# Attention, gated convolution layer and mixture of experts on one core: the weighted sums of every pair of heads as uncut float32 products

## The chip, the cores and the metric

The kernel runs on one core of a Trainium2 chip. The metric is the device time of one execution in microseconds; of several runs the median is given.

## What is computed

Three layers follow one another on 4 batches of 448 positions. Cut to what matters:

```python
attn = softmax(causal(q @ k.T / 8))          # 4 batches x 12 heads, 448 x 448, head size 64
x    = (attn @ v) laid out as 448 x 768      # attention
h    = relu(x @ w_in)                        # 768 -> 1024
x    = (h * sigmoid(conv3(h))) @ w_out       # 1024 -> 768
# 4 experts, each one head of size 64; the two best of each position count
q, k, v = x @ wq[e], x @ wk[e], x @ wv[e]
ye   = softmax(causal(q @ k.T / 8)) @ v @ wo[e]
out += gate(x)[e] * ye
```

Two heads (or two experts) are worked on together and are called a pair. There are 24 pairs in the attention (6 for each batch) and 8 among the experts (2 for each batch), 32 in all. Each has 448 x 448 causal weights a head, of which the lower triangle of blocks is computed.

## The kernel before, in words

`w_out` is folded into the experts' weights, so the products on TensorE are: x by `w_in`, the fold, the experts' q, k, v, the scores, the weighted sums and the output. All but a few of them are "cut": an operand is split into a high part in the type float32r and a low part (`high`, L604 to L608, and `low`, L612), and a product is the sum of three single-pass products, high by high, low by high and high by low (`products`, L951).

For a pair the scores go by four groups of queries (64, 128, 128 and 128 of them; `Q0`, `QN`). `scores` (L680) runs the two heads at once, each in one half of the array's rows, into the two PSUM tiles `sx` and `sy`. VectorE takes the maximum and the mask (L656), ScalarE the exponential (L660), and the weights are divided by their sum (`norms`, L702, L705) in the tile `e`.

Then the weights are turned by TensorE (`tr`, L714, 16 turns of 128 x 128 for a pair) and multiplied by v. There are two ways:

* `weigh_both` (L758), for the first 8 pairs of the attention (`WHOLE_AV`). The weights of both heads stand interleaved in blocks of 64 keys, v stands in a block-diagonal tile (64 keys of one head above 64 keys of the other), and seven uncut float32 products of 448, 384, 320, 256, 192, 128 and 64 columns give both heads at once. The turned weights are copied out of PSUM four times, and the sum is taken out of `po` as a high part and a low part (two instructions).
* `transpose`, `weigh` and `gather` (L772, L784), for the other 16 pairs of the attention and the 8 of the experts. The 64 keys that stand first are stacked for high and low (`a0`), the 384 others are blocks of 128 keys (`a1`, 768 columns). For each head the turned weights are cut into high and low, v too, and seven single-pass products follow (448, 256, 384, 128 columns, then 128 and 256 with 64 columns of v, then 384). High by high and low by high stand in two halves of `po`; ScalarE copies one half out, VectorE adds the other (L784), and `gather` cuts the sum of both heads into high and low again.

What sets the order of all work is a planner (`Plan`): every instruction is entered with the engines that may do it and a cost, the planner gives each a rank by its longest way to the end, adds the noise of the table `SHIFTS` to the ranks in stretches of the plan, and writes the instructions out in the order of its simulated run. TensorE works strictly in that order. `QUOTA`, `SIZE` and `Kind` say how many buffers of a kind there are: `work` is one SBUF area of 11 units of 2 KB for each partition, from which loads, copies and results are taken.

Of the kernel before, what the change touches and what calls it, by code (L numbers as in the profile page):

```python
# [43 lines left out]
PLACE = (0, 1, 4, 2, 5, 3, 6)  # L44
# [4 lines left out]
SIZE = {"t1": 2, "raw": 2, "wt": 2, "wxr": 2, "wraw": 3}  # L49
PAIRS, THOUS, UNITS, SLABS = 18, 4, 11, 3  # L50
QUOTA = {"xs": 7, "qks": 4, "y": 4, "vs2": 2, "w1": 3, "wraw": 1}
# [114 lines left out]
class Plan:  # L166
# [135 lines left out]
    def run(self):  # L302
# [29 lines left out]
        for seed, lo, hi, amp in SHIFTS:  # L332
            for o in self.ops:
                if lo <= begin[o.n] < hi:
                    rank[o.n] += amp * noise(seed, o.n)
# [147 lines left out]
def on_vector2(n):  # L483
# [4 lines left out]
ON = {"a0": ("AV", "A", "A"), "a1": ("AV", "A", "A"), "x high": ("AVG", "VG", "V"), "x low": ("VG", "G", "VG"),  # L488
      "qk high": ("AVG", "AVG"), "qk low": "VG", "v high": ("V", "AG"), "gx": "AG", "w high": "AVG", "w low": "VG"}
# [34 lines left out]
def attention_moe_moe(ctx: ExitStack, tc: tile.TileContext, qk, vv, w_in, cw, w_out, wqk, wvg, wo, out):  # L524
# [38 lines left out]
    blocks = tiles("block", 2, [128, 7, 2, 64], F32)  # L563
    for t in blocks:
        for o in range(2):
            nc.gpsimd.memset(t[HALF[1 - o], :, o], 0.0)
# [6 lines left out]
    thou = Kind(tiles("thou", THOUS, [128, 1024], F32R))  # L573
# [9 lines left out]
    for name, kind, quota in (  # L583
            ("xs", pairs, QUOTA["xs"]), ("g", pairs, 8), ("qks", pairs, QUOTA["qks"]), ("wx", pairs, 12),
            ("y", pairs, QUOTA["y"]), ("q2", pairs, 2), ("k2", pairs, 2),
            ("vs", thou, 2), ("gx", thou, 1), ("vs2", thou, QUOTA["vs2"]), ("w1", slabs, QUOTA["w1"]), ("wraw", half, QUOTA["wraw"]), ("wt", half, 2), ("wxr", half, 2), ("raw", half, 1),
            ("xf", half, 3), ("xc", half, 2), ("cv", half, 3), ("o", half, 3), ("gw", half, 1),
            ("hp", Kind(hps), 2), ("st", Kind(stats), 4),
            ("e", Kind(tiles("e", 2, [128, 2048], F32)), 2), ("vb", bk, 2), ("kb", bk, 1), ("ab", half, 4),
            ("a0", Kind(tiles("a0", 2, [128, S], F32R)), 2), ("a1", Kind(tiles("a1", 1, [128, 2, 768], F32R)), 1),  # L590
            ("vraw", half, 1), ("qw", half, 1),
# [28 lines left out]
    def scores(qk, j, e, turns=False):  # L620
# [13 lines left out]
        def blocked(ap):  # L634
            return ap.rearrange("p (j d) -> p j d", d=64) if turns else ap

# [3 lines left out]
        def ec(o, c):  # L640
            n = Q0[c] + QN[c]
            if turns:
                return e[:QN[c], COL2[c]:COL2[c] + 2 * n].rearrange("p (j o d) -> p j o d", o=2, d=64)[:, :, o]
            return e[:QN[c], COL2[c] + o * n:COL2[c] + o * n + n]

        def kc(o, c):
            n = Q0[c] + QN[c]
            return slice(0, n) if o or turns else slice(S - n, S)

        def weight(o, c):  # L650
# [3 lines left out]
            def mx(_):  # L654
                m = mask[rows, 448 - w:448] if c and (o or turns) else mask[rows, 320:320 + w]
                nc.vector.tensor_tensor_reduce(out=ec(o, c), in0=blocked(bank(o, c)), in1=blocked(m), scale=-0.125, scalar=3.0e38,  # L656
                                               op0=OP.add, op1=OP.min, accum_out=st[rows, 0, c:c + 1])
# [8 lines left out]
        if whole:  # L666
            for o, (qs, kh, r) in enumerate(qk):
                for c in ORDER:
                    w = Q0[c] + QN[c]
                    P.op({"T": 4 * w / 2400}, lambda _, o=o, c=c, w=w, qs=qs, kh=kh: nc.tensor.matmul(  # L670
                        bank(o, c), qs()[:, Q0[c]:Q0[c] + QN[c]], kh()[:, :w // 64], start=True, stop=True), r=r, w=[(sbs[o][c], c)])
                    weight(o, c)
        else:
            q, k, r = qk
            for two in (ORDER[:2], ORDER[2:]):
# [6 lines left out]
                P.op({"T": 0.09 + sum(3 * max(product(Q0[c] + QN[c]), QN[c] / 1200) for c in two)}, mm, r=r,  # L682
# [33 lines left out]
    def transpose(e, p):  # L716


        ph, t0 = 2 if p >= B * NP else int(p >= NP), P.buf("t0")
        a0, a1 = [P.buf("a0") for _ in range(2)], []  # L720
        for c in range(4):
            tr(lambda c=c: t0[:, Q0[c]:Q0[c] + 128], lambda n=COL2[c] + Q0[c] + QN[c]: e[:, n - 64:n + 64],
               [(e, (o, c)) for o in range(2)], [(t0, c)], QN[c])
        src = [(t0, c) for c in range(4)]
        for o in range(2):
            a, own, oth = a0[o], HALF[o], HALF[1 - o]
            P.op(psum_cost(S, ON["a0"][ph]), high(lambda a=a, own=own: a[own], lambda own=own: t0[own, :S]), r=src, w=[(a, 0)])
            P.op({"V": on_vector(S)}, low(lambda a=a, oth=oth: a[oth], lambda own=own: t0[own, :S], lambda a=a, own=own: a[own]),
                 r=src + [(a, 0)], w=[(a, 1)])
        for o in range(2):  # L730
            t1, a = P.buf("t1"), P.buf("a1")
            for i, (c, k) in enumerate(((1, 1), (2, 1), (3, 1), (3, 3), (2, 2), (3, 2))):
                m = COL2[c] + (Q0[c] + QN[c] + Q0[k] if o else Q0[c] - Q0[k])
                tr(lambda t1=t1, n=128 * i: t1[:, n:n + 128], lambda m=m: e[:, m:m + 128], [(e, (o, c))], [(t1, i + 1)])
            src = [(t1, i) for i in range(1, 7)]
            P.op(psum_cost(768, ON["a1"][ph]), high(lambda a=a: a[:, 0], lambda t1=t1: t1[:, :768]), r=src, w=[(a, 0)])
            P.op({"V": on_vector(768)}, low(lambda a=a: a[:, 1], lambda t1=t1: t1[:, :768], lambda a=a: a[:, 0]), r=src + [(a, 0)], w=[(a, 1)])
            a1.append(a)
        return list(zip(a0, a1))

    def weigh_both(e, v, v_r, dst):


        ps = P.buf("po")
        for i, use in enumerate(BLOCKS):
            t, a = P.buf("tb" if i in (1, 2) else "ta"), P.buf("ab")
            n = 0
            for j, col, q in use:
                for c in range((j + 1) // 2, 4):
                    m = COL2[c] + j * 128  # L750
                    tr(lambda t=t, x=col + Q0[c] - q: t[:, x:x + 128], lambda m=m: e[:, m:m + 128], [(e, (o, c)) for o in range(2)],
                       [(t, (j, c))], QN[c])
                n = col + S - q
            P.op(psum_cost(n, "AV"), high(lambda a=a, n=n: a[:, :n], lambda t=t, n=n: t[:, :n]),
                 r=[(t, (j, c)) for j, _, _ in use for c in range((j + 1) // 2, 4)], w=[(a, 0)])
            for j, col, q in use:
                P.op({"T": max(4 * (S - 64 * j) / 2400, 0.214)},
                     lambda _, a=a, j=j, x=col + 64 * j - q, y=col + S - q: nc.tensor.matmul(  # L758
                         ps[:, 64 * j:S], v(PLACE[j]), a[:, x:y], start=j == 0, stop=j == 4), r=[(a, 0)] + v_r, w=[(ps, 0)])
# [3 lines left out]
    def weigh(a, v, v_r, o, xf):  # L763

        a0, a1 = a
        ps, xc = P.buf("po"), P.buf("xc")
        every, vh = slice(0, 128), HALF[0]

        def mm(q, k, m, rhs, key, start=False, stop=False):
            n = m.stop - m.start  # L770
            P.op({"T": product(S - q)},
                 lambda _: nc.tensor.matmul(ps[:n, q:S], v(k, m), rhs(), start=start, stop=stop),  # L772
                 r=key + v_r, w=[(ps, 0)], m=n)

        mm(0, 0, every, lambda: a0[:, :], [(a0, 0), (a0, 1)], start=True)
        mm(192, 2, every, lambda: a1[:, 0, 512:768], [(a1, 0)])
# [439 lines left out]
```

## Time and profile before

| | |
|---|---|
| median of 3 runs | 577.5 us (577.44 to 579.41) |
| the profiled execution | 578.15 us, of which the span of the instructions is 576.4 us |
| PE (matmuls) busy | 554.0 us, 96% |
| DVE busy | 474.1 us, 82% |
| ACT busy | 396.9 us, 69% |
| POOL busy | 179.8 us, 31% |
| DMA queue of the loads | 37.5% of the 16 engines |

PE is TensorE's matmuls, PEld its weight loads, DVE VectorE, ACT ScalarE, POOL GpSimd, SP the queue that issues the DMAs. Matmuls are pipelined: a record lasts from its start until its last result is out, so the records of neighbours overlap, and the pace is read from start to start. An uncut float32 product leaves two matmul records of its width, a cut one a record for each of its parts.

### The profile page before, as it was taken

How to read it: one execution, taken by the hardware profiler on the slowest of the kernel's cores; microseconds unless marked ns; L12 is line 12 of the kernel's file. 1: busy time of each engine (PE TensorE's matmuls, PEld its weight loads, DVE VectorE, ACT ScalarE, POOL GpSimd, SP SyncE). 2: the span in 40 equal slices, each digit the busy share in tenths (PEclk: the TensorE clock that was granted, in tenths of full speed). 3: DMA queues.
4: the chain of work that ended last, by engine and by line, in shares of the span. 5: the costliest groups of instructions: out<-in, count | busy, mean ns of one | idle time of the engine just before them, and what ended most of it. 6: DMA issues, size and time to landing. Idle time of an engine off the chain costs nothing. (4 is left out here: it accounts for less than half of the span.)

```text
span 576.4 us, 10560 instructions
## 1 busy us (share of the span) xinstructions
PE 554.0 (96%) x3549; PEld 474.3 (82%) x3552; DVE 474.1 (82%) x1318; ACT 396.9 (69%) x1033; POOL 179.8 (31%) x236
## 2 busy tenths in 40 slices
PE   8899999899999999999998999999999899999896
PEld 4688888788789998899897878899888778999775
DVE  5996796799997499986799998973999999845883
ACT  3794563377996496863699998953877978634663
POOL 3141201021541274500249766402337452000010
PEclk9999999999999999999999999999989999999999
DMA  9653504865475011546023263650022414610042
GB/s 264 215 150 102 181 1 130 277 177 196 155 266 134 0 51 55 172 161 209 2 54 99 70 215 100 221 193 1 1 66 86 141 54 164 219 55 2 17 134 97
DMA packets 44086, 70.45 MB, mean 122 GB/s; under 512 B 12672, under 2 KB 35072, under 8 KB 44032
## 3 DMA queue, kind: packets, MB, share of 16 engines
q1 hardware_dynamic: 44032, 69.78, 37.5%
q8 instruction: 28, 0.46, 0.3%
q14 instruction: 26, 0.21, 0.1%
HBM read 56.40 MB, written 13.37 MB: 121 GB/s over the span
## 5 line engine op out<-in xcount | busy, mean ns | idle before, releaser
L951 PE MATMUL pf<-pair,slab 128*128 128x448 f32 (+2 forms) x984 | 217.3, 367 | 4.6 <-DVE wqks L612 2.1
L951 PEld LDWEIGHTS pf<-pair,slab 128*128 128x128 f32 x984 | 171.8, 188 | 25.0 <-DVE wqks L612 2.8
L660 ACT ACTIVATE e<-e,stat 128x320 f32<-128x320 f32 (+3 forms) x256 | 127.2, 499 | 24.2 <-DVE stat L656 23.4
L714 PE MATMUL t<-ident,e 128*128 128x128 f32 (+1 forms) x512 | 86.1, 279 | 3.5 <-DVE e L705 1.1
L951 PE MATMUL pf<-pair,wqks 128*128 128x448 f32 x384 | 80.5, 368 | 0.0
L612 POOL TENSOR_TENSOR pair<-work,pair 128x448 fp32r<-128x448 f32 (+1 forms) x55 | 66.3, 1214 | 45.4 <-DVE pair L606 29.0
L612 DVE TENSOR_TENSOR a<-t,a 64x448 fp32r<-64x448 f32 (+1 forms) x96 | 75.5, 787 | 4.8 <-ACT a L604 2.7
L951 PEld LDWEIGHTS pf<-pair,wqks 128*128 128x128 f32 x384 | 71.7, 188 | 6.4 <-DVE pair L612 0.2
L714 PEld LDWEIGHTS t<-ident,e 128*128 128x128 f32 (+1 forms) x512 | 60.2, 140 | 19.7 <-issue 4.4
L604 ACT ACTIVATE a<-t 64x448 fp32r<-64x448 f32 (+1 forms) x96 | 64.2, 673 | 17.0 <-PE t L714 11.6
L772 PE MATMUL po<-a,thou 128*128 128x384 f32 (+5 forms) x336 | 62.8, 310 | 2.4 <-DVE work L784 1.4
L656 DVE CUSTOM_DVE_ANT_0 e<-sx,mask 128x448 f32<-128x448 f32 (+3 forms) x128 | 51.7, 413 | 1.8 <-PE sy L680 0.8
L656 DVE CUSTOM_DVE_ANT_0 e<-sy,mask 128x192 f32<-128x192 f32 (+3 forms) x128 | 51.2, 414 | 2.4 <-PE sy L680 1.2
L772 PEld LDWEIGHTS po<-a,thou 128*128 128x128 f32 (+1 forms) x336 | 47.0, 175 | 6.9 <-DVE work L784 2.8
L680 PE MATMUL sx<-pair,pair 64*128 64x448 f32 (+3 forms) x280 | 50.6, 295 | 0.3 <-DVE stat L656 0.2
L680 PE MATMUL sy<-pair,pair 64*128 64x448 f32 (+3 forms) x280 | 50.2, 294 | 0.2 <-DVE stat L656 0.2
L660 ACT ACTIVATION_READ_ACCUMULATOR e<-e,stat 128x1 f32 (+1 forms) x256 | 48.4, 189 | 0.0
L612 DVE TENSOR_TENSOR pair<-pf,pair 128x448 fp32r<-128x448 f32 (+3 forms) x32 | 15.5, 502 | 38.8 <-ACT pair L604 38.6
L980 DVE SCALAR_TENSOR_TENSOR work<-hp,cws,work 128x448 f32<-128x448 f32 x64 | 45.7, 722 | 1.8 <-ACT work L975 1.1
L702 ACT ACTIVATE e<-e,stat 128x448 f32<-128x448 f32 (+3 forms) x94 | 42.2, 503 | 6.9 <-DVE stat L698 4.1
L680 PEld LDWEIGHTS sx<-pair,pair 64*128 64x128 f32 (+1 forms) x280 | 40.2, 172 | 6.2 <-DVE stat L656 1.5
L951 PE MATMUL pf<-wvs,pair 128*128 128x260 f32 x288 | 43.2, 295 | 0.4 <-DVE thou L612 0.4
(118 smaller groups left out, 872.7 us busy)
## 6 DMA issues: line engine op xcount, KB each, us to landing
slab<-w_scratch SPq DMA_DIRECT2D x24, 768.0 KB, 4.5
work<-in_w_out SPq DMA_DIRECT2D x8, 768.0 KB, 4.9
work<-in_w_in SPq DMA_DIRECT2D x8, 768.0 KB, 5.8
w_scratch<-slab SPq DMA_DIRECT2D x8, 768.0 KB, 4.3
out<-work SPq DMA_DIRECT2D x24, 224.0 KB, 2.0
slab<-wo_scratch SPq DMA_DIRECT2D x6, 768.0 KB, 4.5
work<-in_vv SPq DMA_DIRECT2D x16, 256.0 KB, 2.9
work<-in_qk SPq DMA_DIRECT2D x17, 224.0 KB, 4.2
```

The source lines that it names most:

```text
L604: nc.scalar.activation(dst(), src(), AF.Copy)
L612: return lambda e: engine(e).tensor_sub(dst(), src(), f32(h()))
L656: nc.vector.tensor_tensor_reduce(out=ec(o, c), in0=blocked(bank(o, c)), in1=blocked(m), scale=-0.125, scalar=3.0e38, op0=OP.add, op1=OP.mi ...
L660: nc.scalar.activation(ec(o, c), ec(o, c), AF.Exp, bias=st[rows, 0, c:c + 1], scale=-1.0, accum_out=st[rows, 1, c:c + 1])
L680: nc.tensor.matmul(bank(o, c), q(s)[own, Q0[c]:Q0[c] + QN[c]], k(t)[own, kc(o, c)], start=i == 0, stop=i == 2)
L702: nc.scalar.activation(ec(o, c), ec(o, c), AF.Copy, scale=st[:QN[c], 3, c:c + 1])
L714: P.op({"T": TURN}, lambda _: nc.tensor.transpose(dst()[:, :n], src()[:n], ident[:n, :n]), r=r, w=keys)
L772: lambda _: nc.tensor.matmul(ps[:n, q:S], v(k, m), rhs(), start=start, stop=stop),
L951: nc.tensor.matmul(out_ap(), a(), b(), start=first, stop=end), r=r, w=[(ps, 0)])
L980: return lambda _: nc.vector.scalar_tensor_tensor(cv[:, :S], hp[:, i:S + i], cws[:, fc, i:i + 1], cv[:, :S], op0=OP.mult, op1=OP.add)
```

## The change

All 32 pairs take one new way, also called `weigh`. `transpose`, the old `weigh`, `gather` and `weigh_both` go.

* The first 64 keys of both heads stay together, as one uncut product of 448 columns with a block-diagonal v (128 rows: 64 keys of one head, 64 of the other).
* The other 384 keys are three blocks of 128 keys for each head. Each block is one uncut float32 product with 64 columns of v, of 384, 128 and 256 moving columns. The two heads write to partitions 0 to 63 and 64 to 127 of `po`, that is, they stand beside each other in the array's columns. These six products are one entry of the plan, which waits for all copies of the weights.
* The turned weights are copied once (448 columns, and three times 512), v isn't cut but loaded straight into its place (three DMAs, no copies), and the sum is taken out of `po` once, as high and low.
* v of the experts is copied from PSUM uncut.
* q and k of all pairs but the first come by the four loads that the cut pairs had (pairs 1 to 7 had one); the first pair's k comes by three loads instead of two, with two POOL memsets.
* The `work` area grows from 11 to 19 units, `thou` (four tiles of 4 KB) gives way to one `gx` tile and six v tiles of 2 KB, `a0` and `a1` go.
* The plan's price for a scores group rises from 0.09 to 0.27 beside its columns, the new entry has `SWITCH` = 0.2, and `SHIFTS` is another table, which can also raise the ranks of a run of entries by a constant: the order of all instructions is new.

```diff
-WHOLE_AV = range(8)
-BLOCKS = (((0, 0, 0),), ((1, 0, 64), (5, 384, 320)), ((2, 0, 64), (6, 384, 320)), ((3, 0, 192), (4, 256, 192)))
+TILES = (((0, 1, 1), (0, 2, 1), (0, 3, 1), (0, 3, 3)), ((1, 1, 1), (1, 2, 1), (1, 3, 1), (1, 3, 3)), ((0, 2, 2), (0, 3, 2), (1, 2, 2), (1, 3, 2)))
+SWITCH = 0.2
...
-PAIRS, THOUS, UNITS, SLABS = 18, 4, 11, 3
+PAIRS, VALUES, UNITS, SLABS, EN = 18, 6, 19, 3, 2
...
+    def weigh(e, v, v_r, dst):
+        ps, n0 = P.buf("po"), P.buf("ab")
+        t = P.buf("ta")
         for c in range(4):
+            tr(lambda c=c: t[:, Q0[c]:Q0[c] + 128], lambda n=COL2[c] + Q0[c] + QN[c]: e[:, n - 64:n + 64],
+               [(e, (o, c)) for o in range(2)], [(t, c)], QN[c])
+        P.op(psum_cost(S, "AV"), high(lambda: n0[:, :S], lambda: t[:, :S]), r=[(t, c) for c in range(4)], w=[(n0, 0)])
+        ab = []
+        for i, use in enumerate(TILES):
+            t, a = P.buf("ta" if i == 2 else "tb"), P.buf("ab")
+            for j, (o, c, k) in enumerate(use):
                 m = COL2[c] + (Q0[c] + QN[c] + Q0[k] if o else Q0[c] - Q0[k])
+                tr(lambda t=t, n=128 * j: t[:, n:n + 128], lambda m=m: e[:, m:m + 128], [(e, (o, c))], [(t, j)])
+            P.op(psum_cost(512, "AV"), high(lambda a=a: a[:, :], lambda t=t: t[:, :]), r=[(t, j) for j in range(4)], w=[(a, 0)])
+            ab.append(a)
+        P.op({"T": 4 * S / 2400}, lambda _: nc.tensor.matmul(ps[:, :S], v[:, 0].rearrange("p o d -> p (o d)"), n0[:, :S], start=True, stop=False),
+             r=[(n0, 0)] + v_r, w=[(ps, 0)])
+        def rest(_):
+            for k, part in ((1, lambda o: ab[o][:, :384]), (3, lambda o: ab[o][:, 384:]), (2, lambda o: ab[2][:, 256 * o:256 * o + 256])):
+                for o, own in enumerate(HALF):
+                    nc.tensor.matmul(ps[own, Q0[k]:S], v[:, k, o], part(o), start=False, stop=k == 2)
+        P.op({"T": 4 * 768 / 2400 + SWITCH}, rest, r=[(a, 0) for a in ab] + v_r, w=[(ps, 0)])
         P.op(psum_cost(S, "AV"), high(lambda: dst[:, 0], lambda: ps[:, :S]), r=[(ps, 0)], w=[(dst, 0)])
         P.op({"V": on_vector(S)}, low(lambda: dst[:, 1], lambda: ps[:, :S], lambda: dst[:, 0]), r=[(ps, 0), (dst, 0)], w=[(dst, 1)])
...
+    def values(p):
+        vb = P.buf("vs")
+        for o in range(2):
+            P.op(dma_cost(16384, 256), load(lambda o=o: vb[HALF[o], 0, o], vv[p, HALF[o], 0, o]), w=[(vb, o)])
+        P.op(dma_cost(196608, 1536), load(lambda: vb[:, 1:], vv[p, :, 1:]), w=[(vb, 2)])
+        return vb, [(vb, i) for i in range(3)]
```

## Rows read from the trace of the kernel before

**Rows 1.** The page: busy time of the engines; the DMA queue; the loads of v.

```profile
PE 554.0 (96%) x3549; PEld 474.3 (82%) x3552; DVE 474.1 (82%) x1318; ACT 396.9 (69%) x1033; POOL 179.8 (31%) x236
...
q1 hardware_dynamic: 44032, 69.78, 37.5%
...
work<-in_vv SPq DMA_DIRECT2D x16, 256.0 KB, 2.9
```

**Rows 2.** Busy time by window: us, then PE, PEld, DVE, ACT, POOL busy, clock, DMA.

```profile
250.00:300.00 50.00, 50.00 (x327) 45.31 (x325) 39.30 (x104) 32.16 (x78) 10.06 (x17) 1.00 0.29 96
300.00:350.00 50.00, 47.32 (x351) 40.80 (x352) 47.43 (x159) 48.02 (x136) 37.75 (x48) 1.00 0.37 119
...
400.00:450.00 50.00, 47.06 (x359) 41.25 (x357) 44.74 (x134) 38.94 (x111) 21.89 (x30) 0.97 0.14 45
```

**Rows 3.** The chain that ended last: start, us, what; a long run of cut products.

```profile
485.73 37.70 PE pf L951 x186
```

**Rows 4.** Timeline of PE: start, us, line, shape, count; an uncut pair, then turns.

```profile
120.93 3.30 PE L758 MATMUL po<-work,block 128*128 128x448 f32 x14
123.94 3.74 PE L951 MATMUL pf<-pair,slab 128*128 128x448 f32 x17
...
164.21 1.04 PE L714 MATMUL t<-ident,e 128*128 128x128 f32 x8
```

**Rows 5.** Groups of PE by form: count, busy us, mean ns of a record, idle before.

```profile
L951 PE MATMUL pf<-pair,slab 128*128 128x448 f32 x696 | 159.8, 375 | 2.5 <-ACT hp L969 0.7 <-DVE pair L606 0.7 <-ACT work L604 0.7
L951 PE MATMUL pf<-pair,wqks 128*128 128x448 f32 x384 | 80.5, 368 | 0.0
L714 PE MATMUL t<-ident,e 128*128 128x128 f32 x480 | 80.3, 279 | 3.5 <-DVE e L705 1.1 <-DVE a L612 1.1 <-POOL e L705 0.7
...
L951 PE MATMUL pf<-wvs,pair 128*128 128x260 f32 x288 | 43.2, 295 | 0.4 <-DVE thou L612 0.4
...
L951 PE MATMUL pf<-pair,slab 128*128 128x512 f32 x144 | 39.9, 412 | 2.1 <-DVE wqks L612 2.1
```

**Rows 6.** Timeline of PE: one head's cut sum, then a visit of the scores.

```profile
304.19 1.08 PE L772 MATMUL po<-a,thou 128*128 128x448 f32 x7
305.11 1.24 PE L951 MATMUL pf<-wvs,pair 128*128 128x260 f32 x9
306.28 0.41 PE L680 MATMUL sx<-pair 64*128 64x320 f32 x1
306.28 0.41 PE L680 MATMUL sy<-pair 64*128 64x320 f32 x1
306.53 0.30 PE L680 MATMUL sx<-pair,pair 64*128 64x320 f32 x1
...
306.68 0.31 PE L680 MATMUL sx<-pair,pair 64*128 64x320 f32 x1
...
307.02 0.27 PE L680 MATMUL sx<-pair,pair 64*128 64x192 f32 x1
...
307.23 0.33 PE L714 MATMUL t<-ident,e 128*128 128x128 f32 x1
```

**Rows 7.** The page's costliest groups: cutting the turned weights, busy us and mean ns.

```profile
L612 DVE TENSOR_TENSOR a<-t,a 64x448 fp32r<-64x448 f32 (+1 forms) x96 | 75.5, 787 | 4.8 <-ACT a L604 2.7
...
L604 ACT ACTIVATE a<-t 64x448 fp32r<-64x448 f32 (+1 forms) x96 | 64.2, 673 | 17.0 <-PE t L714 11.6
```

**Rows 8.** Groups by form: sums out of `po` (cut, uncut), and an uncut copy.

```profile
L784 DVE TENSOR_TENSOR work<-po,work 64x448 f32<-64x448 f32 x48 | 29.4, 613 | 6.8 <-ACT work L604 6.0
L604 ACT ACTIVATE work<-po 64x448 f32<-64x448 f32 x48 | 25.9, 540 | 13.9 <-PE po L772 11.7 <-issue 1.4
...
L604 ACT ACTIVATE work<-t 128x512 f32<-128x512 f32 x15 | 8.5, 593 | 3.3 <-PE t L714 2.0 <-PE po L758 0.7 <-DVE work L606 0.6
...
L612 DVE TENSOR_TENSOR pair<-po,pair 128x448 fp32r<-128x448 f32 x8 | 4.9, 616 | 0.1
...
L604 ACT ACTIVATE pair<-po 128x448 fp32r<-128x448 f32 x6 | 3.3, 543 | 4.7 <-PE po L758 4.7
```

More of the change, by code (lines that the diff above doesn't have):

```diff
@@ L617, in attention_moe_moe, with scores @@
     NORM = {}
-    def scores(qk, j, e, turns=False):
+    def scores(qk, j, e):
         whole = isinstance(qk, list)
@@ L647, in kc @@
             n = Q0[c] + QN[c]
[L648 removed]
+            return slice(0, n) if o else slice(S - n, S)
         def weight(o, c):
@@ L654, in mx @@
             def mx(_):
-                m = mask[rows, 448 - w:448] if c and (o or turns) else mask[rows, 320:320 + w]
-                nc.vector.tensor_tensor_reduce(out=ec(o, c), in0=blocked(bank(o, c)), in1=blocked(m), scale=-0.125, scalar=3.0e38,
+                m = mask[rows, 448 - w:448] if c and o else mask[rows, 320:320 + w]
+                nc.vector.tensor_tensor_reduce(out=ec(o, c), in0=bank(o, c), in1=m, scale=-0.125, scalar=3.0e38,
                                                op0=OP.add, op1=OP.min, accum_out=st[rows, 0, c:c + 1])
@@ L680, in mm @@
                                 nc.tensor.matmul(bank(o, c), q(s)[own, Q0[c]:Q0[c] + QN[c]], k(t)[own, kc(o, c)], start=i == 0, stop=i == 2)
-                P.op({"T": 0.09 + sum(3 * max(product(Q0[c] + QN[c]), QN[c] / 1200) for c in two)}, mm, r=r,
+                P.op({"T": 0.27 + sum(3 * max(product(Q0[c] + QN[c]), QN[c] / 1200) for c in two)}, mm, r=r,
                      w=[(sbs[o][c], c) for c in two for o in range(2)])
@@ L787, in gather, with prepare @@
-    def gather(xf, dst, ph):
-        both = [(xf, 0), (xf, 1)]
-        P.op(copy_cost(S, ON["x high"][ph]), high(lambda: dst[:, 0], lambda: xf[:, :S]), r=both, w=[(dst, 0)])
-        P.op(two_cost(S, ON["x low"][ph]), low(lambda: dst[:, 1], lambda: xf[:, :S], lambda: dst[:, 0]), r=both + [(dst, 0)], w=[(dst, 1)])
     turned = ((lambda ap: ap[:, :384].rearrange("p (b c) -> p b c", b=3), lambda ap: ap[:, 64:].rearrange("p (b c) -> p b c", b=3)[:, ::-1]),
               (lambda ap: ap[:, 384:], lambda ap: ap[:, :64]))
-    def prepare(p, ph, turn):
+    def prepare(p, ph):
@@ L803, in both @@
             return raw[:, :2 * S].rearrange("p (a s) -> p a s", a=2)
-        if turn:
-            P.op(dma_cost(229376, 1792), load(lambda: raw[:, :S], qk[p, :, 0]), w=[(raw, 0)], hold=[hi, lo])
-            P.op(dma_cost(114688, 1792), load(lambda: raw[64:, S:2 * S], qk[p, 64:, 1]), w=[(raw, 1)])
-            for i, (d, q) in enumerate(turned):
-                P.op(dma_cost(86016 - 57344 * i, 512 - 256 * i), load(lambda d=d: d(raw[:64, S:2 * S]), q(qk[p, :64, 1])), w=[(raw, 2 + i)])
-        else:
-            P.op(dma_cost(458752), load(both, qk[p]), w=[(raw, i) for i in range(4)], hold=[hi, lo])
+        P.op(dma_cost(229376, 1792), load(lambda: raw[:, :S], qk[p, :, 0]), w=[(raw, 0)], hold=[hi, lo])
+        P.op(dma_cost(114688, 1792), load(lambda: raw[64:, S:2 * S], qk[p, 64:, 1]), w=[(raw, 1)])
+        for i, (d, q) in enumerate(turned):
+            P.op(dma_cost(86016 - 57344 * i, 512 - 256 * i), load(lambda d=d: d(raw[:64, S:2 * S]), q(qk[p, :64, 1])), w=[(raw, 2 + i)])
         src = [(raw, i) for i in range(4)]
@@ L827, in prepare_whole, with side @@
         P.op(dma_cost(229376, 1792), load(lambda: qw[:, :S], qk[p, :, 0]), w=[(qw, 0)])
+        def side(o):
+            return kb[:, o * S:(o + 1) * S]
         for o in range(2):
-            P.op(dma_cost(114688, 256), load(lambda o=o: kb[HALF[o], :, o], qk[p, HALF[o], 1].rearrange("p (j d) -> p j d", d=64)), w=[(kb, o)])
-        return [(lambda: qw[:, :S], lambda o=o: kb[:, :, o], [(qw, 0), (kb, o)]) for o in range(2)]
-    def values(p, ph):
-        raw, vs = P.buf("vraw"), P.buf("vs")
-        def whole():
-            return raw[:, :].rearrange("p (c o d) -> p c o d", c=4, o=2)
-        P.op(dma_cost(262144, 2048), load(whole, vv[p]), w=[(raw, 0)], hold=[vs])
-        def part(i):
-            return vs[:, :].rearrange("p (c s d) -> p c s d", c=4, d=64)[:, :, i:4:2]
-        P.op(copy_cost(512, ON["v high"][ph]), high(lambda: part(0), whole), r=[(raw, 0)], w=[(vs, 0)])
-        P.op(two_cost(512), low(lambda: part(1), whole, lambda: part(0)), r=[(raw, 0), (vs, 0)], w=[(vs, 1)])
-        return vs, [(vs, 0), (vs, 1)]
+            P.op({"G": 0.4}, lambda _, o=o: nc.gpsimd.memset(side(o)[HALF[1 - o]], 0.0), w=[(kb, ("z", o))])
+        for i, (d, q) in enumerate(turned):
+            P.op(dma_cost(86016 - 57344 * i, 512 - 256 * i), load(lambda d=d: d(side(0)[:64]), q(qk[p, :64, 1])), w=[(kb, (0, i))])
+        P.op(dma_cost(114688, 1792), load(lambda: side(1)[64:], qk[p, 64:, 1]), w=[(kb, (1, 0))])
+        return [(lambda: qw[:, :S], lambda o=o: side(o), [(qw, 0), (kb, ("z", o)), (kb, (o, 0))] + [(kb, (0, 1))] * (not o)) for o in range(2)]
+    def values(p):
[4 more added lines that the diff above has]
+        return vb, [(vb, i) for i in range(3)]
     def attention(b):
@@ L849, in attention @@
         for p in range(b * NP, (b + 1) * NP):
-            whole = p in WHOLE_AV
-            ops = prepare_whole(p) if p in WHOLE_QK else prepare(p, ph, not whole)
+            ops = prepare_whole(p) if p in WHOLE_QK else prepare(p, ph)
             xs = P.buf("xs")
-            vs, v_r = values_whole(p) if whole else values(p, ph)
+            vs, v_r = values(p)
             e = P.buf("e")
-            scores(ops, 2 * p, e, whole)
-            if whole:
-                weigh_both(e, vs, v_r, xs)
-            else:
-                xf = P.buf("xf")
-                for o, a in enumerate(transpose(e, p)):
-                    weigh(a, lambda k, m, o=o, vs=vs: vs[:, (k * 2 + o) * 128 + m.start:(k * 2 + o) * 128 + m.stop], v_r, o, xf)
-                gather(xf, xs, ph)
+            scores(ops, 2 * p, e)
+            weigh(e, vs, v_r, xs)
             res.append(xs)
@@ L1123, in experts @@
         for pr in range(2):
[L1124 removed]
+            y, e = P.buf("y"), P.buf("e")
             scores(ops[pr], B * H + b * E + 2 * pr, e)
[L1126 to L1129 removed]
+            weigh(e, vs[pr], [(vs[pr], c) for c in (1, 2, 3)] + [(vs[pr], (0, o)) for o in range(2)], y)
             ys.append(y)
```

123 lines of the change are left out of this document (25 added, 98 removed), and 22 rows, old and new, of the table SHIFTS.

## The prediction

> **What bounds the kernel now.** I read the page's busy times first. TensorE's matmuls are busy 96% of the span, against 82% for VectorE and 69% for ScalarE; the loads' queue uses 37.5% of the DMA engines [rows 1]. So TensorE is the bound on average, but busy time overstates it, since records overlap: a cut product of 448 columns lasts 368 to 375 ns [rows 5], and 186 of them in a row took 37.70 us, 0.203 us each [rows 3], or 0.4525 ns a column. So I price TensorE by start to start.
>
> Next, its work at that pace. The 696 and 384 products of 448 columns come to 219 us, the 144 of 512 to 33, the 288 of 260 to 34 [rows 5]. The 480 turns [rows 5] cost 0.109 us each: eight lasted 1.04 us, of which the last record is 0.28 [rows 4, 5], so (1.04 - 0.28) / 7; that is 52 us. A visit of the scores with 320 and 192 columns runs from the end of the nine products before it to the next turn: nine by 0.118 from 305.11 is 306.17, the turn starts at 307.23, so 1.06 us [rows 6]; two visits for each of 31 pairs give some 65 us. The cut sums: one head takes 305.11 - 304.19 = 0.92 us [rows 6], so 1.84 a pair and 44.2 us for 24 pairs. The uncut ones: a whole pair, 14 records, ran from 120.93 to 123.94, 3.01 us [rows 4], so 24.1 us for 8 pairs. That makes 471. Smaller groups (a second kind of 260 columns, last output blocks, turns of `w_out`, fills, the first pair's scores) I put at 50 us at the same paces. So TensorE has about 521 us of work in a span of 576, and some 55 us are waits of all sizes; the idle time that the page shows is 22 of them [rows 1].
>
> Where they are, the windows tell. From 250 to 300 us the matmuls are busy all 50.00 us, with VectorE at 39.3 and ScalarE at 32.2. From 300 to 350, VectorE is at 47.4, ScalarE at 48.0 and TensorE at 47.3; from 400 to 450, VectorE is at 44.7 and TensorE at 47.1, with the granted clock at 0.97 [rows 2]. The waits come where VectorE and ScalarE are nearly full, and those are stretches with cut pairs.
>
> **What leaves VectorE and ScalarE.** Cutting the turned weights takes 75.5 us of VectorE and 64.2 of ScalarE [rows 7], taking the two halves out of `po` 29.4 and 25.9 [rows 8]: 195 us for 24 pairs, 8.1 a pair. In their place come three copies of 512 columns at 0.593, one of 448 and the sum's high part at 0.543 each (on ScalarE; the same kind of pass) and its low part at 0.616 [rows 8]: 3.5 us a pair. So 4.6 x 24 = 112 us of these engines' 871 go, and the cutting of v and the `gather` steps, partly on POOL, besides. For the 8 uncut pairs nothing here changes: four copies and two passes as before.
>
> **What TensorE pays.** The turns stay at 16 a pair. The uncut pace is 3.01 us for 14 records, 3584 record columns [rows 4]: 0.84 ns for each. The first product of a pair is 2 x 448 x 0.84 = 0.75 us. The other six: one head alone is 2 x 768 x 0.84 = 1.29 us. How two heads beside each other in the columns behave no row shows. The nearest are the scores, two heads in two halves of the rows: `sx` and `sy` start within 0.01 us and the pair then takes 0.15 us for 320 columns [rows 6], the time of one. But there the program takes the halves in turn, record by record; here an uncut product is two records of the same half, one behind the other, then two of the other half. If starts keep the program's order, the first head's second record runs beside the second head's first, and the second head's second beside the next product's first. With widths 384, 128 and 256 that gives 2048 record columns in place of 1536, 1.72 us. One behind the other entirely it is 2.58. I take 1.72, by the order in the code, and keep 1.29 and 2.58 as ends.
>
> Coming and going costs too. The scores start 0.11 us after the pace of the products before them would have it, their first pair takes 0.25 in place of 0.15, and the last one is followed after 0.21, against the 0.09 that 192 columns take [rows 6]: 0.3 us a visit. For column halves the rows have another end: a head's cut sum has two products with only 64 columns of v among seven, and its 1984 columns at 0.4525 make 0.90 of the 0.92 measured [rows 6], so next to nothing. I take 0.3, since here as in the scores two parts of the array run at once. The Trainium skill (TensorEngine Tiling, Key Properties) says that changing the tiling mode drains TensorE, which speaks for the dearer end; by that rule the total stays as below, and without it, it would be 10 us less.
>
> So a new pair is 0.75 + 1.72 + 0.3 = 2.77 us, 32 pairs 88.6, against 68.3 now: **20 us more** for TensorE.
>
> **What comes back.** With 4.6 us less a pair of 8.1, VectorE in the full windows falls to about where it is from 250 to 300, where TensorE doesn't wait [rows 2]. The last sum's way to the output loses a ScalarE pass (0.540) and a VectorE pass (0.613) [rows 8]. There are fewer points where TensorE waits for a single step: per pair three copies before one entry, not cutting steps between two heads, and `po` is given free once, not twice. I take half of the 55 us, **27 us**; the ends are 10 us (little but the page's idle time in full windows and the tail: 2.7 + 2.9 [rows 2] and a few more) and 40 us.
>
> **What is moved.** SP's queue gets 46 more issues: v in three DMAs rather than one for 16 pairs (four for 8), q and k in four rather than one for 7 pairs, one more for the first k. They are hidden as long as the six v tiles and 19 units let loads go early: a load of v now lands in 2.9 us and the queue is at 37.5% [rows 1]. Without that cover a pair's first sum would wait up to those 2.9 us. The wait added is that of the six products for all four copies; behind it in TensorE's order stands whatever the plan put there, and it is one copy long, 0.59 us [rows 8], if the plan left no turns or products in between. The third group of turns waits for the first copy out of `ta`, beside eight turns (0.87 us), so it is hidden; without them it costs 0.54 a pair. The two memsets and the larger tiles cost nothing on the path: POOL is busy 31% [rows 1].
>
> **The sum.** The profiled execution took 578.15 us, 0.65 above the median; its span of 576.4 becomes 576.4 + 20 - 27 = 569.4, and with the same difference to the median of 577.5 the forecast is **570.5 us**. Of this kernel a measurement can tell about 0.5%, 2.9 us, from no change.
>
> **The rivals.**
> *Fully side by side.* The six products take 1.29 us, with visits 2.34 a pair, 74.9 in all, 6.6 more than now: 577.5 + 6.6 - 27 = 557. For it: the scores' halves cost the time of one [rows 6]. Against it: the order of the records. The Trainium skill (TensorE: Matmul & The Clock Gate, Part 3) says that small products in distinct column groups run concurrently just as in row groups; it doesn't say it of uncut float32.
> *One behind the other.* The column halves of uncut products don't overlap. Then a pair is 0.75 + 2.58 + 0.3 = 3.63 us, 116.2 in all, 48 more: 577.5 + 48 - 27 = 598, slower. It decides from the point where the six products take 1.9 us, at which TensorE's rise eats up the 27 us. For it: no row shows column halves at work. That is also the case that the change doesn't do what it says.
> *The waits stay.* TensorE waits because its own order leaves it nothing to do, not for VectorE; six products held behind their last copy take the place of the cutting steps, at up to 0.59 us a pair. Then 10 us come back: 577.5 + 20 - 10 = 588. For it: the clock and PE lose in 400 to 450 us with ScalarE at only 38.9 [rows 2]. Against it: the full stretch from 300 to 350.
>
> **How the numbers follow.** Forecast 0.40 (its own range 562 to 581), fully side by side 0.27, the waits stay 0.20, one behind the other 0.13. Faster takes nearly all of the side-by-side case and some 0.28 of the forecast's 0.40: 0.55. Same takes 0.08 of the forecast and some of the waits' case, 0.15. Slower has the rest, 0.30. The range goes from 553 (side by side, with a little more back) to 590 (waits stay) and leaves out one behind the other and the far ends.
>
> **What would show it.** In the new trace the six products should span about 1.7 us from the first to the next other work, with starts of the second head's records beside the first head's second ones; 1.3 or 2.6 would be the rivals. The groups a<-t at L604 and L612 should be gone and VectorE's share should fall to about 70%. The windows that now hold 47 us of matmuls should hold over 49. The forecast is wrong if TensorE's pace of six products is off by over 0.4 us, 13 us in all, or if idle time of TensorE stays at 22 us.

## The result, and the profile after

The changed kernel takes 555.1 us (median of 4 runs, 554.8 to 555.7) against 578.5 us of the kernel before in the same runs: 0.960 of it, with a 95% interval of 0.957 to 0.962. The forecast was 570.5 us, with 553 to 590 as the range. The direction was right; the gain was 23 us where 7 were forecast, and the time is that of the rival "fully side by side", 557 us.

The page of the profiled execution, its head and the busy times:

```profile
span 553.6 us, 10262 instructions
...
PE 546.8 (99%) x3552; PEld 442.5 (80%) x3552; DVE 400.0 (72%) x1231; ACT 344.8 (62%) x965; POOL 104.3 (19%) x143
```

Against [rows 1], VectorE has 74 us less, ScalarE 52 and POOL 75.5, and TensorE's idle time fell from 576.4 - 554.0 = 22.4 us to 553.6 - 546.8 = 6.8. TensorE is busy 99%. That still overstates its work, since records overlap and since the 99% include the fillers, products without use that both kernels put where TensorE would stand still.

The busy times by window, in the columns of [rows 2]:

```profile
100.00:150.00 50.00, 50.00 (x329) 40.47 (x326) 46.91 (x121) 43.42 (x118) 17.91 (x20) 1.00 0.67 221
150.00:200.00 50.00, 50.00 (x351) 42.66 (x349) 34.28 (x115) 31.69 (x99) 6.65 (x8) 1.00 0.28 82
...
250.00:300.00 50.00, 49.92 (x369) 40.34 (x368) 33.37 (x134) 29.64 (x94) 9.60 (x12) 1.00 0.13 39
300.00:350.00 50.00, 50.00 (x336) 39.22 (x335) 39.33 (x133) 39.57 (x116) 12.85 (x18) 1.00 0.54 170
...
400.00:450.00 50.00, 49.56 (x373) 36.90 (x372) 42.37 (x166) 37.27 (x118) 11.25 (x16) 1.00 0.27 88
```

The granted clock is 1.00 in all of them. The windows don't hold the same work as before, but the fullest one for VectorE and ScalarE in [rows 2] had 47.4 and 48.0 us and left TensorE at 47.3; now the same stretch has 39.3 and 39.6, and TensorE is busy for all 50.00. From 100 to 150 us, however, VectorE is at 46.9 and ScalarE at 43.4, and TensorE is busy for all 50.00 there too: nearly full engines don't by themselves make it wait.

One pair's sums in the timeline of TensorE (start, us, line, shape, count): the product of 448 columns, turns, the six products, then the scores:

```profile
307.92 0.92 PE L727 MATMUL po<-work,block 128*128 128x448 f32 x2
308.68 1.39 PE L708 MATMUL t<-ident,e 128*128 128x128 f32 x9
310.00 1.52 PE L733 MATMUL po<-work,block 128*64 128x384 f32 x12
311.44 0.41 PE L674 MATMUL sx<-pair 64*128 64x320 f32 x1
```

The first product takes 308.68 - 307.92 = 0.76 us, as forecast (0.75). The six take 311.44 - 310.00 = 1.44 us until the next work starts, where 1.72 and the leaving were forecast; in all 32 pairs they take 1.445 to 1.448. One head's 1536 record columns alone are 1.29 us at the pace of [rows 4], so the two heads lie side by side almost from end to end, and 0.15 us is all that the mode costs inside and at the end. Coming adds some 0.09: the turn before the six is followed after 0.20 us where a turn takes 0.109 (a line of it stands with the run head by head). A pair is 0.76 + 1.44 + 0.09 = 2.29 us, 32 pairs are 73.3, and TensorE pays 5 us more than the 68.3 of before, not 20.

The groups that took the place of [rows 7] and [rows 8] (count, busy us, mean ns of one):

```profile
L603 ACT ACTIVATE work<-t 128x512 f32<-128x512 f32 x61 | 34.5, 594 | 15.0 <-PE t L708 7.0 <-DVE work L605 4.8 <-issue 1.8
...
L605 DVE COPY work<-t 128x512 f32<-128x512 f32 x35 | 23.7, 686 | 11.1 <-ACT work L603 5.5 <-PE t L708 5.0 <-DMA block<-in_vv 0.5
...
L611 DVE TENSOR_TENSOR pair<-po,pair 128x448 fp32r<-128x448 f32 x32 | 19.9, 621 | 15.0 <-ACT pair L603 14.4
...
L603 ACT ACTIVATE work<-t 128x448 f32<-128x448 f32 x23 | 12.5, 543 | 23.3 <-PE t L708 20.6 <-PE t L879 1.4 <-issue 1.2
...
L603 ACT ACTIVATE pair<-po 128x448 fp32r<-128x448 f32 x19 | 10.3, 543 | 10.6 <-PE po L733 9.7 <-PE sy L674 0.8
...
L605 DVE CAST pair<-po 128x448 fp32r<-128x448 f32 x13 | 8.1, 621 | 7.6 <-PE po L733 7.6
...
L605 DVE COPY work<-t 128x448 f32<-128x448 f32 x11 | 6.8, 623 | 3.1 <-PE t L708 2.9
```

Together they are 115.8 us for 32 pairs, 3.6 a pair (forecast 3.5), where a cut pair took 8.1.

So the sum comes out as +5 for TensorE and, since the whole is -23, about -28 of waits (forecast -27). The 28 is what is left over, not a measurement. An estimate without the prices agrees with it: counted from the starts of all matmul records (by how much a step is longer than the median step of its kind, where that is over 40 ns), the waits are 63 us before and 40 after; the fillers and the time after the last product's start are another 4 us less, so 27 in all. One term was wrong, by 15 us. Two questions were left for the chip: why the heads lie side by side although an uncut product's two records stand one behind the other in the program, and what brought the 28 us back.

### The profile page after: what moved, and what is told of

It is laid out like the page before. It is cut to its first block, busy times and chain, and to the rows that moved or that the text cites. A ratio compares the mean times of both kernels' runs of the same rounds, so it can differ in the third digit from the quotient of the medians.

```text
span 553.6 us, 10262 instructions
## 1 busy us (share of the span) xinstructions
PE 546.8 (99%) x3552; PEld 442.5 (80%) x3552; DVE 400.0 (72%) x1231; ACT 344.8 (62%) x965; POOL 104.3 (19%) x143
## 4 chain that ended last, share of the span: by engine, by line
PE 89%; DVE 6%; DMA 2%; SPq 1%; issue 1%; ACT 1%; DVEq 0%; ACTq 0%
PE pf L879 52%; PE t L708 11%; PE sx L674 9%; PE po L733 8%; PE po L727 4%; PE pf L986 1%; DVE work L605 1%; DVE e L699 1%; DMA work<-in_w_out 1%; SPq L614 1%; DVE e L650 1%; PE pf L1081 1%; DMA work<-in_qk 1%; PE sy L674 1%; PE pf L582 1%
## 5 line engine op out<-in xcount | busy, mean ns | idle before, releaser
L654 ACT ACTIVATE e<-e,stat 64x64 f32<-64x64 f32 (+3 forms) x256 | 127.4, 503 | 22.7 <-DVE stat L650 22.4
L603 ACT ACTIVATE work<-t 128x512 f32<-128x512 f32 (+1 forms) x84 | 46.5, 580 | 38.3 <-PE t L708 27.6
L650 DVE CUSTOM_DVE_ANT_0 e<-sx,mask 128x320 f32<-128x320 f32 (+3 forms) x128 | 51.6, 416 | 18.0 <-PE sy L674 14.6
L611 POOL TENSOR_TENSOR pair<-work,pair 128x448 fp32r<-128x448 f32 (+1 forms) x32 | 41.9, 1320 | 64.7 <-ACT pair L603 41.1
L908 DVE SCALAR_TENSOR_TENSOR work<-hp,cws,work 128x448 f32<-128x448 f32 x64 | 43.4, 687 | 14.1 <-ACT work L903 13.4
L699 POOL TENSOR_SCALAR e<-e,stat 128x448 f32<-128x448 f32 (+3 forms) x46 | 26.5, 586 | 123.5 <-ACT e L654 63.3
L733 PE MATMUL po<-work,block 128*64 128x128 f32 (+2 forms) x384 | 48.5, 388 | 0.0
L674 PEld LDWEIGHTS sy<-pair,pair 64*128 64x128 f32 (+1 forms) x280 | 40.5, 172 | 0.2
L605 DVE COPY work<-t 128x512 f32<-128x512 f32 (+1 forms) x46 | 30.1, 671 | 14.1 <-PE t L708 7.9
L879 PE MATMUL pf<-wvs,pair 128*128 128x260 f32 x288 | 38.8, 289 | 0.0
L733 PEld LDWEIGHTS po<-work,block 128*64 128x64 f32 x384 | 22.5, 136 | 19.2 <-issue 15.5
```

Source lines behind the costliest of these rows:

```text
L603: nc.scalar.activation(dst(), src(), AF.Copy)
L605: nc.vector.tensor_copy(dst(), src())
L611: return lambda e: engine(e).tensor_sub(dst(), src(), f32(h()))
L650: nc.vector.tensor_tensor_reduce(out=ec(o, c), in0=bank(o, c), in1=m, scale=-0.125, scalar=3.0e38, op0=OP.add, op1=OP.min, accum_out=st[ro ...
L654: nc.scalar.activation(ec(o, c), ec(o, c), AF.Exp, bias=st[rows, 0, c:c + 1], scale=-1.0, accum_out=st[rows, 1, c:c + 1])
L674: nc.tensor.matmul(bank(o, c), q(s)[own, Q0[c]:Q0[c] + QN[c]], k(t)[own, kc(o, c)], start=i == 0, stop=i == 2)
```

## The experiments

**Head by head.** Does the order of the six products matter?

```diff
-            for k, part in (...):
-                for o, own in enumerate(HALF):
+            for o, own in enumerate(HALF):
+                for k, part in (...):
                     nc.tensor.matmul(ps[own, Q0[k]:S], v[:, k, o], part(o), ...)
```

> Edit: the six products of a pair go head by head, the three of the first head and then the three of the second, in place of the two heads in turn. Theory A, the two column halves overlap as far as the two heads' products are near each other in the program's order: now only the last product of the first head can overlap with the first of the second, so the six take about 2.4 us instead of 1.35 (2816 record columns at 0.84 ns), 1.0 us more a pair, 33 us in all: 588 us. Theory B, each half of the columns runs on its own, however far ahead its work stands: the six stay at 1.35 us and the time at 555 us.

Measured: 577.5 us, 22 above the changed kernel; neither theory. The timeline of TensorE at the first pair (start, us, line, shape, count):

```profile
29.63 2.21 PE L733 MATMUL po<-work,block 128*64 128x384 f32 x12
31.77 0.73 PE L879 MATMUL pf<-pair,slab 128*128 128x512 f32 x2
```

The turn before them:

```profile
29.43 0.27 PE L708 MATMUL t<-ident,work 128*128 128x128 f32 x1
```

The records that run between 30.300 and 30.330 us, by form (count, busy us, mean ns, idle):

```profile
L733 PE MATMUL po<-work,block 128*64 128x384 f32 x1 | 0.5, 486 | 0.0
L733 PE MATMUL po<-work,block 128*64 128x128 f32 x1 | 0.3, 273 | 0.0
```

and between 30.330 and 30.336:

```profile
L733 PE MATMUL po<-work,block 128*64 128x384 f32 x2 | 0.9, 512 | 0.0
L733 PE MATMUL po<-work,block 128*64 128x128 f32 x1 | 0.3, 273 | 0.0
```

The six take 31.77 - 29.63 = 2.14 us, between 1.44 and 2.4, and 32 x 0.70 are the 22 us. The program's order is 384, 128, 256 of the first head and then 384 of the second, two records each. At 30.33, 0.70 us after the start, the first head's third record (its first of 128) has started, and within 6 ns of it one more of 384 starts. That can only be the second head's: it has passed the first head's second record of 128 and both of 256. It had not started earlier, while four or five records stood before it. So the starts do not keep the program's order when the records belong to different halves of the columns, but a record passes only so many. (Each record has a weight load of its own, so the limit may lie there as well; the runs don't tell the two apart.) This is where my forecast went wrong, and the sentence ahead of the prediction that TensorE works strictly in the plan's order doesn't hold for such records. The Trainium skill (TensorE: Matmul & The Clock Gate, Part 3) says that matmuls start and end strictly in the program's order; for the starts of records in different column halves this run shows otherwise, and the measurement decides. What the same section says of small products in distinct column groups, that they run at the same time, holds here for uncut float32 too.

**Two products ahead.** How far may one half run ahead?

```diff
+            for use in ((one, three), (two,)):     # 384 and 128 columns, then 256
                 for o, own in enumerate(HALF):
+                    for k, part in use:
                         nc.tensor.matmul(ps[own, Q0[k]:S], v[:, k, o], part(o), ...)
```

> Edit: the order of the six products is first head 384 and 128 columns, second head 384 and 128, then 256 of each. Read from the run head by head: there the second head's first record started just after the first head's third, ahead of three records that stand before it in the program. If a half of the columns may run ahead of the other by so much and no more, the second head's first record is now the fourth after the first head's first, so it starts within 0.01 us of it, the six take 1.35 us and the time stays at 555 us. If a record can pass only the second record of the product before it, or if starts keep the program's order, the second head starts 0.37 us late or more, and the six take at least 1.55 us: 562 us or more.

Measured: 555.2 us, and the six take 31.28 - 29.82 = 1.46 us:

```profile
29.82 1.52 PE L735 MATMUL po<-work,block 128*64 128x384 f32 x12
31.28 1.20 PE L881 MATMUL pf<-pair,slab 128*128 128x512 f32 x4
```

Here the second head's first record stands behind three of the first head's that wait, and it starts 0.014 us after the first one. So three records may stand between, as in the run head by head; four and five were too many there.

**Full width.** What are the column halves worth, and is TensorE the bound?

```diff
-                for o, own in enumerate(HALF):
-                    nc.tensor.matmul(ps[own, Q0[k]:S], v[:, k, o], part(o), ...)
+                for o in range(2):
+                    nc.tensor.matmul(ps[:, Q0[k]:S], v[:, k].rearrange("p o d -> p (o d)"), part(o), ...)
```

> Edit: each of the six products uses all 128 columns, with v of both heads as weights, so that the heads can't stand beside each other; this adds one head's weights by the other's v into the sums, so the sums are other ones. If TensorE is the bound and the halves are worth what the trace shows (1.45 us for the six with leaving, about 0.09 for coming; 2 x 1.29 = 2.58 one behind the other, without a visit), a pair takes 1.04 us more, 32 pairs 33 us: 588 us. If TensorE has slack that hides products, or the gain came from VectorE and ScalarE alone: below 565 us.

Measured: 588.4 us, 33 more, as 32 pairs at 1.04 us make. The timeline of TensorE at the second pair has 86.19 - 83.59 = 2.60 us to the start of the next work:

```profile
83.59 2.77 PE L733 MATMUL po<-work,block 128*128 128x384 f32 x12
86.19 0.27 PE L708 MATMUL t<-ident,e 128*128 128x128 f32 x1
```

In these two runs, 22 and 33 us, a microsecond more of TensorE is a microsecond more of the span. Without the halves the change would have lost 10 us to the kernel before: the rival "one behind the other" had the right price (598, of which 32 x 0.3 = 10 us are visits that this form doesn't pay).

**Copies twice, order kept.** Do the waits come back with the load?

```diff
-        P.op(psum_cost(512, "AV"), high(...), ...)
+        P.op(psum_cost(512, "AV"), twice(high(...)), ...)      # the five plain copies of a pair
```

> Edit: each of the five plain copies of a pair (four of turned weights, the sum's high part) is done twice, in the same place of the same order; 32 x (3 x 0.59 + 2 x 0.54) = 92 us of work go back to ScalarE and VectorE, of the 112 us that the change took away; TensorE's work is unchanged. If the waits went because these engines have less to do: 15 to 25 us more, 570 to 580 us, with idle time of TensorE back in the windows where VectorE and ScalarE are full. If they went because of the new order and fewer points of waiting: 560 us or less.

Measured: 596.1 us, 41 more. What TensorE waited for (us in total, times, longest), in this run:

```profile
PE t L708 <- DVE work L605: 9.4, 10, 2.0
PE t L708 <- ACT work L603: 5.9, 12, 1.3
```

and in the changed kernel:

```profile
PE t L708 <- DVE work L605: 0.9, 3, 0.4
```

The turns wait for the copies that free their PSUM tile. 41 us is far above the 15 to 25 that were expected from the load, so the next run lets the plan know.

**Copies twice, planned.**

```diff
+        more = lambda cost: {e: 2 * c for e, c in cost.items()}
-        P.op(psum_cost(512, "AV"), twice(...), ...)
+        P.op(more(psum_cost(512, "AV")), twice(...), ...)
```

> Edit: the five copies of a pair are done twice as in the run before, and the plan is told so (their costs are doubled), so that the order is made for it. If the load of VectorE and ScalarE by itself makes the waits: about as slow as with the order kept, 585 to 597 us. If it was that each copy came later than the order assumed, so that TensorE stood in front of it in its fixed order: most of the 41 us go, 558 to 575 us.

Measured: 573.5 us, 18 more than the changed kernel. So of the 41 us, 23 go when the order is made for the longer copies, and 18 are what 92 us of extra copies cost in this order. Scaled to the 112 us that the change took away, that is 22 us. It is one order: orders of the changed kernel itself, without the table, lie between 553 and 562 us (below), against which the copies cost 11 to 20, or 14 to 25 scaled.

**Before, with short low parts.** The reverse test on the kernel before, order kept:

```diff
-            low(lambda a=a: a[:, 1], lambda t1=t1: t1[:, :768], lambda a=a: a[:, 0])
+            low(lambda a=a: a[:, 1, :64], lambda t1=t1: t1[:, :64], lambda a=a: a[:, 0, :64])   # a0 likewise
```

> Edit, on the kernel before: the low parts of the turned weights are computed for 64 columns only (of 768 and of 448), the rest stays zero, so the sums lack most of the low by high products' input; order, TensorE's instructions and all waits stay. VectorE loses 48 x (0.95 - 0.13) + 48 x (0.62 - 0.13) = 63 us. If VectorE's load makes the waits: 8 to 16 us less, 562 to 570 us. If the order and the points of waiting make them: 575 us or more.

Measured: 571.3 us, 0.989 of the kernel before (0.984 to 0.994), 7 us less. Its page:

```profile
PE 554.1 (97%) x3552; PEld 476.7 (83%) x3552; DVE 427.7 (75%) x1318; ACT 397.3 (69%) x1033; POOL 183.2 (32%) x239
```

The page is of an execution of 575.5 us. VectorE is busy 46 us less, not 63: the short passes take 0.22 us and not 0.13, so they save 54, and its other passes took 8 longer. TensorE's work is the same. 571.3 lies just above the range for "VectorE's load makes the waits" and below that for "the order makes them". Scaled to 112 us, 7 for 46 would be 17 us, not far from the 22 above, though the order wasn't made for the shorter steps. So the load counts in the old order too.

**Without the tables.** How much of the gain is the new table of rank noise?

```diff
-SHIFTS = ( ... )
+SHIFTS = ()
```

> Edit, on the changed kernel: the table SHIFTS is empty, so the plan's own order is used. Together with the same edit on the kernel before: if the new table were what brought the waits down, the two kernels without tables would stand within 10 us of each other; if the new way of the weighted sums brings them down under any order, they stay 18 to 28 us apart. Alone I expect 560 to 575 us.

> Edit, on the kernel before: the table SHIFTS is empty. I expect 582 to 597 us, 18 to 28 us above the changed kernel without its table, if the way of the sums is what counts; within 10 us of it if the table is.

Measured: 553.3 us for the changed kernel (553.1 to 553.6), 588.4 for the kernel before. They stand 35 us apart, more than with their tables (23) and more than the 18 to 28 expected: the table was worth 10 us to the kernel before, and the changed one is 1.8 us faster without it. This is the fastest version of the study, and in part luck: four other orders without the table, below, take 559.3 to 562.3 us. Against all five the kernel before stands 26 to 35 us higher, 29 on the mean. So the new table isn't what brought the gain; what else changed with the way of the sums (the area, the loads, the price of a scores group) is still in it.

**24 pairs uncut in the old way.** The kernel before, without its table:

```diff
-WHOLE_AV = range(8)
+WHOLE_AV = range(24)
```

> Edit, on the kernel before without its table: all 24 pairs of the attention take its own uncut way (block-diagonal v of 64 keys a head, no column halves); the experts stay cut. TensorE pays 16 x (3.01 - 1.84) = 18.7 us more. The two kernels without tables stand 588.4 to 553.3; with 5 us more work on TensorE in the second, 40 us of waits went with 24 pairs' cutting, 1.67 us a pair. If that is so, 16 pairs give 27 back: 588.4 + 18.7 - 27 = 580 us. If the waits went for other reasons (the larger area, the v tiles): 595 us or more.

Measured: 592.3 us, between the two forecasts. If TensorE's 18.7 us more are paid at that price, 588.4 + 18.7 - 592.3 = 14.8 us of waits went with 16 pairs' cutting, 0.9 a pair and not 1.67. For 24 pairs that is 22 us, the same as from the copies done twice, but again from one order on each side. The edit also changes the loads of these pairs (q and k in one instead of four, v in four instead of one). Of the rest of the 40 us between the two plain kernels some 6 are the lucky order of 553.3 us; this run doesn't say where the others come from.

**The work area, the price in the plan, and other orders.** First the area alone, then the measured price of the six products:

```diff
-PAIRS, VALUES, UNITS, SLABS, EN = 18, 6, 19, 3, 2
+PAIRS, VALUES, UNITS, SLABS, EN = 18, 6, 12, 3, 2
```

> Edit, on the changed kernel without its table: the work area has 12 units in place of 19, about what it had before. If the larger area brought waits down by letting loads and copies go earlier: 560 us or more. If it didn't: 550 to 557 us.

```diff
-SWITCH = 0.2
+SWITCH = 0.26
```

> Edit, on the changed kernel without its table: SWITCH is 0.26, the cost of the six products as measured (1.45 us with leaving, 0.09 for coming, against 1.48 in the plan). The order becomes another. 551 to 555 us; nothing that depends on the plan's 4% error in this one price.

Measured: 570.7 us with 12 units, 562.3 with the other price. The second was a miss: a price changed by 0.06 us makes another order, and that alone costs 9 us. So one order can't judge the area, and three more prices were tried, each with 19 units and with 12:

```diff
-SWITCH = 0.2
+SWITCH = 0.14      # 0.23, 0.3
```

> Edit, on the changed kernel without its table: SWITCH 0.14, 19 units; it serves to give another order. Orders with 19 units so far: 553.3 and 562.3 us. If these two span what an order does, 551 to 564 us.

> Edit: SWITCH 0.14 with 12 units in the work area. If the larger area is worth 8 us or more under any order: 566 to 576 us, above every order with 19 units. If the 570.7 us of the first run with 12 units was its order: 553 to 563 us.

> Edit: SWITCH 0.23, 19 units, another order. 551 to 564 us, as for the first of this kind.

> Edit: SWITCH 0.23 with 12 units. 566 to 576 us if the area is worth 8 us or more under any order; 553 to 563 us if not.

> Edit: SWITCH 0.3, 19 units, another order. 551 to 564 us, as for the other two of this kind.

> Edit: SWITCH 0.3 with 12 units. 566 to 576 us if the area is worth 8 us or more under any order; 553 to 563 us if not.

| price of the visit in the plan | 19 units | 12 units |
|---|---|---|
| 0.14 | 561.0 | 568.2 |
| 0.20 | 553.3 | 570.7 |
| 0.23 | 559.3 | 571.9 |
| 0.26 | 562.3 | not run |
| 0.30 | 560.9 | 561.4 |

The four pairs differ by 7.2, 17.4, 12.6 and 0.5 us, 9 on the mean; one of the four shows nothing, so "8 us or more under any order" is refuted. Where the time goes, the windows of the first run with 12 units tell (the columns of [rows 2]; of an execution of 574.1 us):

```profile
0.00:50.00 50.00, 43.59 (x235) 31.56 (x236) 37.40 (x104) 27.71 (x69) 11.98 (x28) 0.93 0.69 207
...
100.00:150.00 50.00, 47.72 (x317) 37.01 (x318) 46.59 (x129) 36.05 (x102) 19.39 (x14) 0.97 0.52 173
150.00:200.00 50.00, 45.15 (x259) 36.25 (x258) 37.46 (x93) 33.70 (x90) 16.63 (x13) 0.93 0.49 164
```

The last two were full in the changed kernel, with its table and without (49.95 and 50.00): they are the stretch where the loads and conversions of the first layers' weights share the area with the pairs. With 12 units TensorE loses 7 us in them and the granted clock falls to 0.97 and 0.93. The clock missing in the three windows is 50 x (0.07 + 0.03 + 0.07) = 8.5 us, of the 21 by which this execution is longer than 553.3; the pair that shows nothing, at 0.30, has a clock of 1.00 with 12 units too. With an order spread of 9 us, "some 9 us" for the area is a mean, not a rule for any one order.

**Two entries.** Did the wait of the six products for all four copies cost anything?

```diff
-        P.op({"T": 4 * 768 / 2400 + SWITCH}, rest, r=[(a, 0) for a in ab] + v_r, w=[(ps, 0)])
+        P.op({"T": 4 * 512 / 2400 + SWITCH}, some((384 and 128 columns)), r=[(a, 0) for a in ab[:2]] + v_r, w=[(ps, 0)])
+        P.op({"T": 4 * 256 / 2400 + SWITCH}, some((256 columns)), r=[(ab[2], 0)] + v_r, w=[(ps, 0)])
```

> Edit, on the changed kernel without its table: the entry of the six products is split into two, the four of 384 and 128 columns, which need only the first three copies, and the two of 256, so that TensorE may do other work between. Where other work stands between, a second visit of the column halves is paid, about 0.2 to 0.3 us a pair, 6 to 9 us in all. If the wait for all four copies cost TensorE nothing: 556 to 562 us. If the wait was a cost, the split wins it back: 553 us or less.

Measured: 561.0 us, 8 above the plain order. In the trace other work stands between in 16 of the 32 pairs. There the two parts take 1.02 and 0.58 us in place of 1.45, and with 0.09 more to come that is 0.24 a second visit, 4 us in all; the other 4 us are the order, and 561 is also where other orders of the unsplit entry lie. It didn't win anything back. There was next to nothing to win: among the waits listed for TensorE's matmuls in the changed kernel, 4.5 us in all, none is before the six products, and what comes before them runs on into them with no more than the 0.1 us of the visit in 30 of the 32 pairs.

## Why the prediction was wrong in size, and how its other terms stand

* **The step that failed** is "If starts keep the program's order, the first head's second record runs beside the second head's first". The rule was wrong: records of the other column half pass up to three that stand before them. The six products took 1.44 us with leaving, against 1.72 and 0.3 for the visit; a pair 2.29 against 2.77; 32 pairs 73.3 against 88.6. That is 15 of the 15 us by which the forecast was too high. The choice of 1.72 came from the order of the code; no row had shown two column halves at work.
* **The visit** was put at 0.3 us by the scores. For the column halves the rows give 0.09 to come and about 0.15 inside and to leave, 0.24. The Trainium skill (TensorEngine Tiling (Array Packing), Key Properties) says that a change of mode drains TensorE. The trace has a gap, but less than a whole drain: head by head the six start at 29.63 us, before the end of the turn at 29.43 + 0.27 = 29.70, an end that is modelled.
* **The first product** (0.75 forecast, 0.76 measured) and the uncut pace held.
* **The load of VectorE and ScalarE**: 3.5 us a pair forecast, 3.6 measured; VectorE fell to 72% where about 70 was said.
* **The waits**: 27 forecast, about 28 came back. The size was right, in part by luck: half of 55 us was a choice and not a sum, and another order of the changed kernel could have been 7 us slower. The reason is right only in part, and argued in part. Three runs give 17 to 22 us for the lighter copies, each from one order. The larger work area, which I had put at no cost and no gain, gives some 9 us on the mean of four orders. The two add to 26 to 31, against 28 here and 34 without the tables (29 against the mean of five orders, and TensorE's 5); the difference is within what an order does.
* **What is moved**: right. Of the idle time before the copies above, 0.5 us is put down to the loads of v; 46 more issues on SP cost nothing that can be seen.
* **The rivals**: "fully side by side" is what happened, at 557 forecast and 555.1 measured, and had 0.27. "The waits stay" is refuted by the time, 555 and not 588, and by TensorE's idle time, 6.8 us and not 22.4. "One behind the other" was refuted by the trace and its price was confirmed by the run at full width.

What stays open: how far exactly the area's gain depends on the order; what the new price of a scores group in the plan (0.27 for 0.09), the v tiles and the load taken off POOL (75.5 us less) did, which no run takes apart; and whether there is an order below 553 us. By the prediction's sum TensorE has 521 + 5 us of work, so some 28 us of waits are still in the span, and the 99% don't show that there is no room.

## What to carry to other kernels

Where TensorE is near its limit, compare two ways of a product by all that they ask of the other engines: here 5 us more of TensorE came with some 28 us less of waits, most of which the runs put down to the passes on VectorE and ScalarE that cutting a freshly made operand into high and low parts costs. When several products share the array, put those of different column halves within three records of each other, and measure the stretch before assuming that it runs in order. When an order is made by a planner, a change of one price can move the time by 1.6% (553.3 to 562.3 us), so judge a part of a change by several orders.

## What the runs showed of the hardware that was not expected

* Matmul records of different column halves pass each other: a record started ahead of three earlier ones of the other half, but not while four or five stood before it; with up to three between them the six products took 1.44 to 1.46 us, with the three products of one half ahead of those of the other 2.14.
* Two halves of the columns with uncut float32 operands run side by side at nearly full pace: 1.44 us, of which 0.15 is for the mode, for what takes about 2.6 at full width.
* With the order of instructions fixed, 92 us of extra copies cost 41 us; with one order made for them, 18.
